# Score copies on the Vector engine: two pairs in one instruction, or each pair alone under a new planning string

## The chip, the cores and the metric

The kernel runs on one core of a Trainium2 chip. The number that counts is the device time of one execution in microseconds: 1544.43 us is the median of three runs before the change (1543.17 to 1547.52). The engines named below are TensorE (PE, its weight loads PEld), VectorE (DVE), ScalarE (ACT), GpSimd (POOL) and the queue of SyncE (SP), from which all transfers are issued.

## The reference

Four residual layers over 2048 tokens of width 512: softmax attention with 32 heads of 16, then a GELU network of width 1376, and both again with the same weights. What matters here is the exponential of the attention scores:

```python
scores = jnp.einsum("bhqd,bhkd->bhqk", q, k) * scale
p = _softmax(scores, axis=-1)
o = jnp.einsum("bhqk,bhkd->bhqd", p, v)
```

For every layer and head that is 2048 x 2048 exponentials. In tiles of 128 keys by 512 queries there are 4096 score tiles over the two attention layers.

## The kernel before, in words

**Units and segments.** The tokens are worked on in units (`build_segments`): four units of 512 queries in the first attention layer (called layer 1 in the code), and three of 512, one of 256 and two of 128 in the second (layer 3). A unit has eight groups of four heads; one unit and one group make a segment. The four heads of a group lie in the four 32-row strips of PE, so that score products (L1536) of four heads run side by side.

**Two ways to the exponential.** `flow_scores` walks over the score tiles. Groups of three and two PSUM banks alternate; ACT exponentiates a group in one instruction (L1521) into `PT`. Beside it, `take_d` and `d_solo` hand single tiles to DVE, only for the key blocks listed in `DK`. DVE adds a constant to the score and stores it as a 16-bit integer (`d_load`, L1628): read as bfloat16 bits, this is a coarse exponential. Its error is averaged out by three more copies of the same bits, shifted by 32, 64 and 96 (`SHIFT`), each multiplied with values scaled by a matching weight (`vs`). A tile on ACT therefore needs one value product (L1741), a tile on DVE four.

**The copies.** Tiles on DVE are collected in pairs (`DBATCH`). `job_d` makes the copies of a pair: first the copy shifted by 32 (L1659, 128x1024), into the second buffer of the pair, then both buffers shifted by 64 in one instruction (L1667, 128x2048), into another pair of buffers from the pool `dp`. In the kernel before, a copy task that is about to be placed looks for a second one of the same kind among those that wait. If there is one and it is ready, both are written as one instruction over two pairs (`d_join`): L1614, 128x2048 in place of two L1659, and L1615, 128x4096 in place of two L1667. For the access patterns of `both` the buffers must lie in one tensor, `bits`: 14 units of `dp` and behind them four that are `OT`, of which one pair is lent to the pool for part of the time (`LENT`). The pool is kept sorted, so that the lowest free pair is taken.

**Who sets the order.** All instructions are laid out before the kernel runs, by a planner (`Sched`) that works with durations written in the code. At each step it takes the pending task that can start first on its engine, by priority and age. A few of its settings change on the way: `Hint.ORDER` is a string with one digit for every four score groups, and each digit picks one of the sets in `MODES`. (`a` and `b` set `POST`, by which `soft` changes the priority of PE work of the GELU network.) `post_prio` gives the priority of what follows a unit's attention: 0.95 for late units, 2.2 for the others, and 0.9499 for the third unit of layer 1. Because the planner places each task where everything before has put the clock, another string gives another order from the first differing step on, on every engine and queue.

**Padding.** After the order is fixed, `refill` walks through it again and puts products with zeros (L1425, L1427, L1429) where PE would stand, so that the clock of PE is kept up.

**What follows a segment.** When the last value product of a segment is in, DVE transposes the sums (L1771), POOL or DVE divide; after eight segments the unit's output projection (L1821), the layer norm, the transposed rows `yT` (L1872), the first product of the network (L1882), one GELU session on ACT (L1934, with a table load on either side) and the second product (L1943) follow, among the score work of the next units. The first two units of layer 3 share one GELU session (`HELD`). The start of layer 3 waits for the scale of its keys (L1228 to L1232) and queries (L1262).

Of the kernel before, what the change touches and what calls it, by code (L numbers as in the profile page):

```python
# [254 lines left out]
class Task:  # L255

    __slots__ = ("eng", "ops", "prio", "cb", "seq", "mate")

    def __init__(self, eng, prio, ops):
        self.eng = eng  # L260
        self.prio = prio
        self.ops = ops
        self.cb = None
        self.seq = 0
        self.mate = None

# [12 lines left out]
class Sched:  # L279
# [80 lines left out]
    def release(self, name, slot):  # L360
        p = self.pools[name]
        if slot in p.retired:
            key = p.retired.pop(slot)
            self.mark(key)
            return
        if p.waiters:
            _, _, cb = heapq.heappop(p.waiters)
            cb(slot)
        else:
            p.free.append(slot)  # L370
            if name == "dp":
                p.free.sort()

# [74 lines left out]
    def run(self):  # L448
        while True:
# [18 lines left out]
            self.pend[t.eng].remove(t)  # L468
            both = None
            if t.mate is not None:  # L470
                lim = max(pick[0], self.P.free["dve"]) + self.LOOK["dve"]
                both = next((o for o in self.pend["dve"] if o.mate is not None and o.mate[0] == t.mate[0] and (o.mate[1] < t.mate[1]) == (o.mate[2] < t.mate[2]) and self.task_ready(o) <= lim), None)
            if both is not None:
                self.pend["dve"].remove(both)
                (fn, reads, writes, same_ok, dur, lat), more = t.ops[0], both.ops[0]
                x, y = sorted((t.mate[1:], both.mate[1:]))
                self.P.op("dve", self.join(t.mate[0], x, y), reads + more[1], writes + more[2], same_ok, dur + more[4] - SHIFT_FIXED, lat)
                for o in sorted((t, both), key=lambda o: o.mate[1:]):
                    o.cb()
            else:  # L480
                for (fn, reads, writes, same_ok, dur, lat) in t.ops:
                    self.P.op(t.eng, fn, reads, writes, same_ok, dur, lat)
                if t.cb is not None:
                    t.cb()
            if t.eng == "dve" and self.after_dve is not None:
# [5 lines left out]
AHEAD = 0.3  # L491
SHIFT_FIXED = 0.15
HOLD_REACH = 1.0
# [15 lines left out]
DBATCH = 2  # L509
DFLY = 4  # L510
DBACK = 2.0
NDP = 14
# [21 lines left out]
DOT = True  # L534
LENT = NDP + 2

# [22 lines left out]
class Builder:  # L559
# [45 lines left out]
    def alloc(self, es):  # L605
# [120 lines left out]
    def otd(self, hg):  # L726

        return [("dp", LENT + (hg - 4) // 2, w) for w in (0, 1)] if DOT and hg >= 4 else []

    def dpu(self, u):  # L730

        return self.bits[:, u, :]

    def dpp(self, u):

        return self.bits[:, u:u + 2, :]

    def both(self, a, b, o=None):

        if o is not None:  # L740
            return self.bits[:, a + o:b + o + 1:b - a, :]
        return self.bits[:, :, :].rearrange("p (u a) n -> p u (a n)", a=2)[:, a // 2:b // 2 + 1:(b - a) // 2, :]

# [866 lines left out]

    def d_join(self, kind, x, y):

        if kind == 1:
            return lambda e: e.tensor_scalar(out=self.both(x[0], y[0], 1), in0=self.both(x[0], y[0], 0), scalar1=float(SHIFT[1]), scalar2=None, op0=ALU.add)  # L1614
        return lambda e: e.tensor_scalar(out=self.both(x[1], y[1]), in0=self.both(x[0], y[0]), scalar1=float(SHIFT[2]), scalar2=None, op0=ALU.add)  # L1615

    def close_batch(self):
# [35 lines left out]
    def job_d(self, bt):  # L1653
# [4 lines left out]
        prio = lambda: 0.15 if not self.left(sg) and sg is self.segs[self.acc_seg] else 0.5 if self.left(sg) < DURGE else 2.5  # L1658
        t = Task("dve", prio(), [I(lambda e: e.tensor_scalar(out=self.dpu(u + 1)[:, 0:N], in0=self.dpu(u)[:, 0:N], scalar1=float(SHIFT[1]), scalar2=None, op0=ALU.add),  # L1659
                                     [("dp", u, w) for w in range(n)], [("dp", u + 1, w) for w in range(n)] + self.dres(u + 1), 0.150 + 0.2605e-3 * N, (), "fast")])  # L1660
        if n == DBATCH:
            t.mate = (1, u, u)
        yield t
        self.d_ready(bt, 1, u + 1, u, range(n))
        v = yield ("get", "dp", sg["i"])
        self.need2 -= 1
        t = Task("dve", prio(), [I(lambda e: e.tensor_scalar(out=self.dpp(v)[:, :, 0:N], in0=self.dpp(u)[:, :, 0:N], scalar1=float(SHIFT[2]), scalar2=None, op0=ALU.add),  # L1667
                                     [("dp", u + i, w) for i in (0, 1) for w in range(n)], [("dp", v + i, w) for i in (0, 1) for w in range(n)] + self.dres(v) + self.dres(v + 1), 0.150 + 0.521e-3 * N, (), "fast")])
        if n == DBATCH:
            t.mate = (2, u, v)  # L1670
        yield t
        for i in (0, 1):
# [391 lines left out]
    def build(self):  # L2064
# [32 lines left out]
        if DOT:  # L2097
            S_.when([("ot", 1, 0, hg) for hg in range(8)], lambda: S_.release("dp", LENT))
            S_.when([("ot", 1, self.NC - 1, hg) for hg in range(8)], lambda: S_.retire("dp", LENT, ("retd", 0)))
            S_.when([("ot", 3, 0, hg) for hg in range(8)], lambda: S_.release("dp", LENT))  # L2100
            S_.when([("ot", 3, len(self.units[3]) - 3, hg) for hg in range(8)], lambda: S_.retire("dp", LENT, ("retd", 1)))
# [3 lines left out]
        S_.join = self.d_join  # L2105
        self.P.spare = lambda: (tuple(range(6)) if self.wide and ("scores_done",) not in S_.done else ()) + ((MISCB,) if MISCB in S_.pools["mb"].free else ())
# [60 lines left out]
```

## Time and profile before

| | |
|---|---|
| median of three runs | 1544.43 us |
| the profiled execution's own time | 1543.17 us |
| its span, first to last instruction | 1541.4 us |
| granted PE clock over the span | 0.998 |
| ACT busy | 1503.9 us (98%) |
| PE busy, zero products included | 1490.7 us (97%) |
| DVE busy | 1446.3 us (94%) |
| POOL busy | 346.7 us (22%) |
| exponentials on ACT (L1521) | 1256 instructions, 1423.3 us |
| loads of score tiles on DVE (L1628) | 982 instructions, 651.6 us |

The page gives busy time, the chain that ended last and the costliest groups of instructions; a group's line reads: line of the kernel, engine, operation, output and input, count, then busy time and mean duration in ns, then the idle time of the engine just before these instructions and who ended it. A view in order of time begins with the start in us and the duration. PE's busy time is modelled, so that a full PE is not one at its peak.

### The profile page before, as it was taken

To read this page: it belongs to the slowest core of one execution; us is meant where nothing else is said; L and a number is where in the kernel's file an instruction comes from. 1 tells how busy PE (TensorE), PEld (TensorE's weight loads), DVE (VectorE), ACT (ScalarE), POOL (GpSimd) and SP (SyncE) were. 2 spreads that over 40 slices of the span, in tenths; PEclk is the share of its full clock that TensorE was granted. 3 is DMA by queue.
4 is the path that set the end of the run, shared out by engine and by line. 5 is a ranking of instruction groups with operands and counts; after the bars stand their busy time and mean duration, and the time that the engine had idled before them with its cause. 6 is when DMAs were issued, how large, how long until landed. Compare 5 with 4: busy or idle time off the path is not lost.

```text
span 1541.4 us, 41484 instructions
## 1 busy us (share of the span) xinstructions
PE 1490.7 (97%) x17809; PEld 491.4 (32%) x17809; DVE 1446.3 (94%) x2653; ACT 1503.9 (98%) x1346; POOL 346.7 (22%) x570
## 2 busy tenths in 40 slices
PE   8999999999999999999999999999999999999998
PEld 3222222232222322222222232222222222343565
DVE  8799999999999999998999898999999998998886
ACT  8999999999999999999999999999999999999997
POOL 3586421100330021301232228320001100011110
PEclk9999999999999999999999999999999999999999
DMA  6662111212312033123562233311011100111221
GB/s 166 115 151 87 35 26 32 53 35 58 80 53 63 17 66 90 50 55 72 124 106 63 65 74 71 58 26 22 22 25 29 29 19 28 43 38 43 70 60 33
DMA packets 212488, 90.57 MB, mean 59 GB/s; under 512 B 182251, under 2 KB 207184, under 8 KB 212304
## 3 DMA queue, kind: packets, MB, share of 16 engines
q1 hardware_dynamic: 212304, 87.92, 25.2%
q8 instruction: 139, 2.28, 0.6%
q14 instruction: 45, 0.37, 0.1%
HBM read 36.81 MB, written 19.48 MB: 37 GB/s over the span
## 4 chain that ended last, share of the span: by engine, by line
ACT 43%; PE 28%; DVE 23%; issue 2%; POOL 2%; DMA 1%; SPq 0%; POOLq 0%; DVEq 0%
ACT PT L1521 40%; DVE dp L1628 10%; PE ps L1536 9%; PE ps L1741 9%; PE ps L1882 3%; PE ps L1943 3%; DVE dp L1667 2%; PE ps L1016 2%; DVE dp L1615 2%; ACT h L1934 1%; DVE dp L1659 1%; DVE dp L1614 1%; DVE accT L1771 1%; PE ps L1429 1%; DVE n L1081 1%
## 5 line engine op out<-in xcount | busy, mean ns | idle before, releaser
L1521 ACT ACTIVATE PT<-ps 128x1536 bf16<-128x1536 f32 (+1 forms) x1256 | 1423.3, 1286 | 24.9 <-PE ps L1536 21.5
L1628 DVE TENSOR_SCALAR dp<-ps 128x512 uint16<-128x512 f32 x982 | 651.6, 680 | 37.9 <-PE ps L1536 34.2
L1536 PE MATMUL ps<-QT,KT 32*128 32x512 bf16 (+2 forms) x5120 | 596.3, 340 | 21.6 <-ACT PT L1521 7.2
L1741 PE MATMUL ps<-PT,V 128*17 128x512 bf16 (+2 forms) x3896 | 487.4, 339 | 1.2 <-issue 1.2
L1741 PE MATMUL ps<-dp,vs 128*17 128x512 bf16 (+2 forms) x3672 | 472.2, 339 | 0.9 <-DVE dp L1667 0.8
L1536 PEld LDWEIGHTS ps<-QT,KT 32*128 32x128 bf16 x5120 | 171.5, 91 | 535.5 <-ACT PT L1521 281.3
L1262 POOL TENSOR_SCALAR QT<-qraw,scl,qbias 128x512 bf16<-128x512 bf16 (+2 forms) x91 | 75.2, 826 | 727.9 <-PE ps L1536 721.6
L1741 PE MATMUL ps<-dp,V 128*17 128x512 bf16 (+2 forms) x1224 | 224.0, 340 | 2.1 <-DVE accT L1771 1.8
L1667 DVE TENSOR_SCALAR dp<-dp 128x2048 uint16<-128x2048 uint16 (+1 forms) x298 | 208.6, 701 | 3.2 <-PE ps L1741 0.7
L1429 PE MATMUL ps<-zw 128*32 128x448 bf16 (+17 forms) x1708 | 169.3, 326 | 1.1 <-DVE dp L1628 1.1
L1741 PEld LDWEIGHTS ps<-dp,vs 128*17 128x17 bf16 x3672 | 123.8, 89 | 120.6 <-issue 87.1
L1741 PEld LDWEIGHTS ps<-PT,V 128*17 128x17 bf16 x3896 | 125.3, 89 | 93.3 <-issue 77.7
L1659 DVE TENSOR_SCALAR dp<-dp 128x1024 uint16<-128x1024 uint16 (+1 forms) x284 | 123.2, 435 | 2.5
L1615 DVE TENSOR_SCALAR dp<-dp 128x4096 uint16<-128x4096 uint16 x98 | 122.6, 1253 | 0.1
L1427 PE MATMUL ps<-zw 32*128 32x444 bf16 (+4 forms) x364 | 113.4, 331 | 0.0
L1882 PE MATMUL ps<-yT,wf 128*128 128x512 bf16 (+5 forms) x440 | 104.5, 343 | 6.1 <-DVE dp L1615 2.2
L1016 PE MATMUL ps<-wqkv,xnT 128*128 128x512 bf16 x336 | 91.4, 382 | 1.0 <-DVE dp L1029 0.2
L1425 PE MATMUL ps<-zw 128*128 128x448 bf16 (+20 forms) x321 | 80.7, 334 | 4.9 <-DVE dp L1628 2.3
L1287 POOL TENSOR_SCALAR vs<-V 128x340 bf16<-128x340 bf16 (+2 forms) x72 | 65.7, 914 | 28.5 <-PE ps L1741 17.4
L1614 DVE TENSOR_SCALAR dp<-dp 128x2048 uint16<-128x2048 uint16 x105 | 71.7, 684 | 0.0
L1741 PEld LDWEIGHTS ps<-dp,V 128*17 128x17 bf16 x1224 | 56.5, 88 | 40.7 <-issue 21.4
L1429 PEld LDWEIGHTS ps<-zw 128*32 128x32 bf16 x1708 | 59.4, 95 | 23.2 <-DVE dp L1628 3.7
(201 smaller groups left out, 1055.0 us busy)
## 6 DMA issues: line engine op xcount, KB each, us to landing
vs<-vs_scr SPq DMA_DIRECT2D x64, 255.0 KB, 2.7
wf<-in_B_w_dram SPq DMA_DIRECT2D x90, 128.0 KB, 2.6
q_scr<-qk SPq DMA_DIRECT2D x20, 256.0 KB, 2.1
k_scr<-qk SPq DMA_DIRECT2D x12, 256.0 KB, 2.0
out_dram<-xres SPq DMA_DIRECT2D x16, 128.0 KB, 1.7
vs_scr<-vs SPq DMA_DIRECT2D x8, 255.0 KB, 3.0
xres<-in_A_x_dram SPq DMA_DIRECT2D x7, 256.0 KB, 5.4
v_scr<-vst SPq DMA_DIRECT2D x12, 136.0 KB, 1.7
```

The costliest lines, as they stand in the source:

```text
L1016: yield Task("pe", prio if c0 == 0 else min(prio, HINT.LIN2), [I(lambda e, c=c: e.matmul(self.ps[:, b, :], lhsT=xnT[:, c, :], rhs=self.wqk ...
L1427: fn = lambda e: e.matmul(self.ps[:, b, 0:w], lhsT=self.zw[32 * p:32 * p + 32, 0:128], rhs=self.zw[32 * p:32 * p + 32, 0:w], start=st, sto ...
L1429: fn = lambda e: e.matmul(self.ps[32 * p:32 * p + 32, b, 0:w], lhsT=self.zw[:, 0:32], rhs=self.zw[:, 0:w], start=st, stop=st, skip_group_c ...
L1521: S_.submit(Task("act", 1e-5 * gi, [I(lambda e, pt=pt, n=n, b0=b0: e.activation(out=self.PT[:, pt:pt + n, :], in_=self.ps[:, b0:b0 + n, :] ...
L1536: return [I(lambda e, kb=kb, i=i: e.matmul(self.ps[:, b, i * W:(i + 1) * W], lhsT=self.KT[32 * hp:32 * hp + 32, hg, kb * 128:(kb + 1) * 12 ...
L1614: return lambda e: e.tensor_scalar(out=self.both(x[0], y[0], 1), in0=self.both(x[0], y[0], 0), scalar1=float(SHIFT[1]), scalar2=None, op0= ...
L1615: return lambda e: e.tensor_scalar(out=self.both(x[1], y[1]), in0=self.both(x[0], y[0]), scalar1=float(SHIFT[2]), scalar2=None, op0=ALU.add)
L1628: self.S_.submit(Task("dve", 0.0, [I(lambda e: e.tensor_scalar(out=self.dpu(u)[:, w * 512:(w + 1) * 512], in0=self.ps[:, b, :], scalar1=BI ...
L1659: t = Task("dve", prio(), [I(lambda e: e.tensor_scalar(out=self.dpu(u + 1)[:, 0:N], in0=self.dpu(u)[:, 0:N], scalar1=float(SHIFT[1]), scal ...
L1667: t = Task("dve", prio(), [I(lambda e: e.tensor_scalar(out=self.dpp(v)[:, :, 0:N], in0=self.dpp(u)[:, :, 0:N], scalar1=float(SHIFT[2]), sc ...
L1741: ops.append((nth[j, sh] + 0.1 * i, I(lambda e, hp=hp, v=v, ap=ap[:, i * W:(i + 1) * W], first=first and i == 0, W=W: e.matmul(self.ps[32 ...
L1882: yield Task("pe", self.soft(pr if c0 == 0 else min(pr, HINT.LIN2)) if y0 == 0 else pr, [I(lambda e, c=c: e.matmul(self.ps[0:M, b, 0:W], l ...
```

## The change

Pairs are no longer joined: each copy task becomes one instruction (L1659 or L1667 alone), and `mate`, the search for a second task, `d_join` and `both` go. `OT` is a tensor of its own again, the lent pair has number 14 instead of 16, and the pool hands pairs out in the order in which they came free. The third unit of layer 1 has priority 0.95 like the fourth, and `soft` under `POST` 1 lowers every priority under 2, not only those from 0.95. `ORDER` is another string; the first 20 digits are the same.

```diff
             self.pend[t.eng].remove(t)
-            both = None
-            if t.mate is not None:
-                lim = max(pick[0], self.P.free["dve"]) + self.LOOK["dve"]
-                both = next((o for o in self.pend["dve"] if o.mate is not None and o.mate[0] == t.mate[0] and (o.mate[1] < t.mate[1]) == (o.mate[2] < t.mate[2]) and self.task_ready(o) <= lim), None)
-            if both is not None:
-                self.pend["dve"].remove(both)
-                (fn, reads, writes, same_ok, dur, lat), more = t.ops[0], both.ops[0]
-                x, y = sorted((t.mate[1:], both.mate[1:]))
-                self.P.op("dve", self.join(t.mate[0], x, y), reads + more[1], writes + more[2], same_ok, dur + more[4] - SHIFT_FIXED, lat)
-                for o in sorted((t, both), key=lambda o: o.mate[1:]):
-                    o.cb()
-            else:
-                for (fn, reads, writes, same_ok, dur, lat) in t.ops:
-                    self.P.op(t.eng, fn, reads, writes, same_ok, dur, lat)
-                if t.cb is not None:
-                    t.cb()
+            for (fn, reads, writes, same_ok, dur, lat) in t.ops:
+                self.P.op(t.eng, fn, reads, writes, same_ok, dur, lat)
+            if t.cb is not None:
+                t.cb()
...
             p.free.append(slot)
-            if name == "dp":
-                p.free.sort()
...
-    ORDER = '6178431488213042224130050030302033700020011073304410301330955937002083398440030130002450200030130000b900020559554104005025041510300311442533255001003000050793300000071500903503010300030000033043004332000204000034300444003074442000033000003055000733004099594093074053909900398000448301001020b9419803824b00195100a1010'
+    ORDER = '617843148821304222410024330100010322200010402005142300045935291731905421304450012300445404028299551400009505333207404304200030002302391015000030510104040320034300330030059090225910306350630422003320070322304130078057891b143300430303032703000430001459928b9001b338492908900532301308540020000009440105408040a010010a0211'
...
-        self.bits = t("dp", [128, NDP + 4, 1024], U16)
-        self.dp = self.bits[:, 0:NDP, :]
+        self.dp = t("dp", [128, NDP, 1024], U16)
...
-        self.OT = self.bits[:, NDP:NDP + 4, :].bitcast(BF16).rearrange("p u (a n) -> p (u a) n", n=512)
+        self.OT = t("OT", [128, 8, 512], BF16)
...
-    def d_join(self, kind, x, y):
-
-        if kind == 1:
-            return lambda e: e.tensor_scalar(out=self.both(x[0], y[0], 1), in0=self.both(x[0], y[0], 0), scalar1=float(SHIFT[1]), scalar2=None, op0=ALU.add)
-        return lambda e: e.tensor_scalar(out=self.both(x[1], y[1]), in0=self.both(x[0], y[0]), scalar1=float(SHIFT[2]), scalar2=None, op0=ALU.add)
...
-        t = Task("dve", prio(), [I(lambda e: e.tensor_scalar(out=self.dpu(u + 1)[:, 0:N], in0=self.dpu(u)[:, 0:N], scalar1=float(SHIFT[1]), scalar2=None, op0=ALU.add),
+        yield Task("dve", prio(), [I(lambda e: e.tensor_scalar(out=self.dpu(u + 1)[:, 0:N], in0=self.dpu(u)[:, 0:N], scalar1=float(SHIFT[1]), scalar2=None, op0=ALU.add),
...
-        return 1.1 if HINT.POST == 1 and 0.95 <= pr < 2 else 0.95 if HINT.POST == 2 and pr > 2 else pr
+        return 1.1 if HINT.POST == 1 and pr < 2 else 0.95 if HINT.POST == 2 and pr > 2 else pr
...
-        return 0.9499 if (L, qc) == (1, self.NC - 2) else 0.95 if L == 1 and qc >= self.NC - 2 or L == 3 and qc >= LATE3 else 2.2
+        return 0.95 if L == 1 and qc >= self.NC - 2 or L == 3 and qc >= LATE3 else 2.2
```

More of the change, by code (lines that the diff above doesn't have):

```diff
@@ L255 @@
 class Task:
-    __slots__ = ("eng", "ops", "prio", "cb", "seq", "mate")
+    __slots__ = ("eng", "ops", "prio", "cb", "seq")
     def __init__(self, eng, prio, ops):
@@ L264, in __init__ @@
         self.seq = 0
-        self.mate = None
 def I(fn, reads=(), writes=(), dur=0.3, same_ok=(), lat=None):
@@ L491 @@
 AHEAD = 0.3
-SHIFT_FIXED = 0.15
 HOLD_REACH = 1.0
@@ L534 @@
 DOT = True
-LENT = NDP + 2
 HELD = {(3, 0): (3, 1)}
@@ L726, in otd @@
     def otd(self, hg):
-        return [("dp", LENT + (hg - 4) // 2, w) for w in (0, 1)] if DOT and hg >= 4 else []
+        return [("dp", NDP + (hg - 4) // 2, w) for w in (0, 1)] if DOT and hg >= 4 else []
     def dpu(self, u):
-        return self.bits[:, u, :]
+        return self.dp[:, u, :] if u < NDP else self.OT[:, 2 * (u - NDP) + 4:2 * (u - NDP) + 6, :].rearrange("p a n -> p (a n)").bitcast(U16)
     def dpp(self, u):
[L736 to L742, printed above, removed]
+        return self.dp[:, u:u + 2, :] if u < NDP else self.OT[:, 4:8, :].rearrange("p a n -> p (a n)").bitcast(U16).rearrange("p (u n) -> p u n", u=2)
     def dres(self, s):
@@ L1658, in job_d @@
         prio = lambda: 0.15 if not self.left(sg) and sg is self.segs[self.acc_seg] else 0.5 if self.left(sg) < DURGE else 2.5
-        t = Task("dve", prio(), [I(lambda e: e.tensor_scalar(out=self.dpu(u + 1)[:, 0:N], in0=self.dpu(u)[:, 0:N], scalar1=float(SHIFT[1]), scalar2=None, op0=ALU.add),
+        yield Task("dve", prio(), [I(lambda e: e.tensor_scalar(out=self.dpu(u + 1)[:, 0:N], in0=self.dpu(u)[:, 0:N], scalar1=float(SHIFT[1]), scalar2=None, op0=ALU.add),
                                      [("dp", u, w) for w in range(n)], [("dp", u + 1, w) for w in range(n)] + self.dres(u + 1), 0.150 + 0.2605e-3 * N, (), "fast")])
-        if n == DBATCH:
-            t.mate = (1, u, u)
-        yield t
         self.d_ready(bt, 1, u + 1, u, range(n))
@@ L1666, in job_d @@
         self.need2 -= 1
-        t = Task("dve", prio(), [I(lambda e: e.tensor_scalar(out=self.dpp(v)[:, :, 0:N], in0=self.dpp(u)[:, :, 0:N], scalar1=float(SHIFT[2]), scalar2=None, op0=ALU.add),
+        yield Task("dve", prio(), [I(lambda e: e.tensor_scalar(out=self.dpp(v)[:, :, 0:N], in0=self.dpp(u)[:, :, 0:N], scalar1=float(SHIFT[2]), scalar2=None, op0=ALU.add),
                                      [("dp", u + i, w) for i in (0, 1) for w in range(n)], [("dp", v + i, w) for i in (0, 1) for w in range(n)] + self.dres(v) + self.dres(v + 1), 0.150 + 0.521e-3 * N, (), "fast")])
-        if n == DBATCH:
-            t.mate = (2, u, v)
-        yield t
         for i in (0, 1):
@@ L2097, in build @@
         if DOT:
[L2098 to L2101, printed above, removed]
+            S_.when([("ot", 1, 0, hg) for hg in range(8)], lambda: S_.release("dp", NDP))
+            S_.when([("ot", 1, self.NC - 1, hg) for hg in range(8)], lambda: S_.retire("dp", NDP, ("retd", 0)))
+            S_.when([("ot", 3, 0, hg) for hg in range(8)], lambda: S_.release("dp", NDP))
+            S_.when([("ot", 3, len(self.units[3]) - 3, hg) for hg in range(8)], lambda: S_.retire("dp", NDP, ("retd", 1)))
         S_.when([("qt", 0)], lambda: S_.spawn(self.flow_scores(), 0.0))
@@ L2104, in build @@
         S_.after_dve = self.d_solo
-        S_.join = self.d_join
         self.P.spare = lambda: (tuple(range(6)) if self.wide and ("scores_done",) not in S_.done else ()) + ((MISCB,) if MISCB in S_.pools["mb"].free else ())
```

## The prediction

> **What bounds the kernel now.** I read the page's shares first, then the chain, then the groups by form, then the Vector engine's order of time, and last the stretches in which the Scalar engine stands still. The page's head, slices and chain:
>
> ```profile
> span 1541.4 us, 41484 instructions
> PE 1490.7 (97%) x17809; PEld 491.4 (32%) x17809; DVE 1446.3 (94%) x2653; ACT 1503.9 (98%) x1346; POOL 346.7 (22%) x570
> ...
> ACT 43%; PE 28%; DVE 23%; issue 2%; POOL 2%; DMA 1%; SPq 0%; POOLq 0%; DVEq 0%
> ```
>
> Three engines are almost full, and the chain changes hands between them. No single engine can be relieved alone: each of the 4096 score tiles is exponentiated either by ACT or by DVE, so DVE time that is lost becomes ACT time. The groups by form say what a tile costs on either side:
>
> ```profile
> L1521 ACT ACTIVATE PT<-ps 128x1536 bf16<-128x1536 f32 x603 | 908.3, 1506 | 18.6 <-PE ps L1536 15.9
> L1521 ACT ACTIVATE PT<-ps 128x1024 bf16<-128x1024 f32 x652 | 699.1, 1083 | 6.3 <-PE ps L1536 5.6
> ...
> L1628 DVE TENSOR_SCALAR dp<-ps 128x512 uint16<-128x512 f32 x982 | 651.6, 680 | 37.9 <-PE ps L1536 34.2
> L1667 DVE TENSOR_SCALAR dp<-dp 128x2048 uint16<-128x2048 uint16 x292 | 205.9, 706 | 3.1 <-PE ps L1741 0.7
> L1615 DVE TENSOR_SCALAR dp<-dp 128x4096 uint16<-128x4096 uint16 x98 | 122.6, 1253 | 0.1
> L1659 DVE TENSOR_SCALAR dp<-dp 128x1024 uint16<-128x1024 uint16 x278 | 121.5, 438 | 2.5
> L1614 DVE TENSOR_SCALAR dp<-dp 128x2048 uint16<-128x2048 uint16 x105 | 71.7, 684 | 0.0
> ```
>
> L1614 and L1615 are the joined copies, L1659 and L1667 the single ones. A mean is not yet the time that the engine gives to an instruction, since neighbours overlap. The Vector engine in order of time (start, duration):
>
> ```profile
> 508.91 0.68 DVE L1614 TENSOR_SCALAR dp<-dp 128x2048 uint16<-128x2048 uint16 x1
> 509.50 0.68 DVE L1628 TENSOR_SCALAR dp<-ps 128x512 uint16<-128x512 f32 x1
> 510.10 0.68 DVE L1667 TENSOR_SCALAR dp<-dp 128x2048 uint16<-128x2048 uint16 x1
> ...
> 512.56 0.42 DVE L1659 TENSOR_SCALAR dp<-dp 128x1024 uint16<-128x1024 uint16 x1
> 512.90 0.69 DVE L1628 TENSOR_SCALAR dp<-ps 128x512 uint16<-128x512 f32 x1
> ```
>
> L1614 begins at 508.91, lasts 0.68, and the next begins at 509.50: an overlap of 0.09. L1659's is 0.08. I take 0.08 off every DVE mean. For ACT, the two exponential forms sum to 1607.4 us, while the page's group, which counts overlapped time once, has 1423.3 for 1256: 0.147 each. So a three-bank activation costs 1.359 us of ACT and a two-bank one 0.936.
>
> **The change part by part.** Durations come from the profiled execution: span 1541.4 us, its own time 1543.17, the lowest of three; the median is 1544.43, 1.3 us above it.
>
> *Unjoining.* Two singles replace each joined copy. L1614: 2 x (0.438 - 0.08) - (0.684 - 0.08) = 0.112 us, 105 times, 11.8 us. L1615: 2 x (0.706 - 0.08) - (1.253 - 0.08) = 0.079, 98 times, 7.7 us. Together 19.5 us more DVE time for the same tiles. The means hold disturbed instances. With the typical ones (0.419 and 0.684 for the singles' medians, 0.683 and 1.217 for the joined) each join is worth 0.071 us, 203 of them 14.4 us. Ends 14.4 and 19.5; I take 19.5, as the instances to come will meet the same neighbours.
>
> [...]
>
> *The new order.* The planner lays out everything anew with the new string, so I counted both instruction listings. DVE loads (L1628) go from 982 to 971; the single copies become 482 and 482 of full width with 7 and 7 half-width ones; no joined ones stay. ACT gets three more three-bank activations and one more two-bank (606 and 653), which are just the 11 tiles. So ACT: 3 x 1.359 + 0.936 = **+5.0 us**. DVE: a tile costs a load of 0.600 and half a pair of copies, (0.358 + 0.626) / 2 = 0.492, so 11 tiles give back 12.0: 19.5 - 12.0 = **+7.5 us** (by the low end, +2.4). By stage the listing loses 7 of the 11 tiles in the first layer's second unit and 4 in the second layer's fifth; the others differ by two at most.
>
> *PE.* An ACT tile needs one value product, a DVE tile four: the listing has 36 fewer, which run four at a time. One takes 0.38 in the trace, 36 / 4 x 0.38 = 3.4 us at most, while consecutive rounds start 0.22 apart, so 2.0. PE is padded with zero products (L1425, L1427, L1429), and the freed time becomes padding or idle. I count 0 and keep -2.0.
>
> *Buffers.* OT leaves the large tensor, the pair on loan from it gets another number, and a free pair is taken in order of release instead of the lowest first. Shapes and strides of the single copies stay, so no duration changes. DVE idles 3.1 us before L1667 in all; the order of reuse can take away at most that or, by the same row, add as much. I take 0, covered by a pool of 8 pairs.
>
> *Priorities.* 0.9499 becomes 0.95 for the first layer's third unit, so that its work ties with the fourth's and falls to the older task. At 681 us the third unit's GELU runs; its second products (L1943) end at 707, while the fourth unit's attention goes on for some 150 us more, so the two rarely meet. The wider condition in soft meets no other priority: the 'a' steps stand at groups 1216 to 1247, where the post work has 0.95 under both texts. Both 0. DMA counts stay at 545 rows of SP and 574 of POOL; their places move with the plan, and nothing is put past them on purpose.
>
> *Waits.* Joined copies also make others wait:
>
> ```profile
> L1741 PEld LDWEIGHTS ps<-dp,vs 128*17 128x17 bf16 x3672 | 123.8, 89 | 120.6 <-issue 87.1 <-DVE dp L1667 6.3 <-DVE dp L1615 5.1
> ```
>
> L1615 shows 5.1 us of weight-load waits, and L1614 4.4 by its own line; the single L1667 has 6.3. Weight loads run ahead of the matmuls, and matmuls behind dp lost 0.9 us in all before this line. Bounds of this gain: 0 and 9.5 us; I take 0, near the 0.9.
>
> *The stalls that a plan happens to have.* ACT's idle time of more than a microsecond in the steady part has three places:
>
> ```profile
> 707.45 16.05 ACT L1521 ACTIVATE PT<-ps 128x1024 bf16<-128x1024 f32 x14 [2.24 <-PE ps L1536]
> ```
> ```profile
> 927.09 12.76 ACT L1521 ACTIVATE PT<-ps 128x1536 bf16<-128x1536 f32 x11 [3.87 <-PE ps L1536]
> ```
> ```profile
> 1397.12 4.63 ACT L1521 ACTIVATE PT<-ps 128x1536 bf16<-128x1536 f32 x4 [2.87 <-PE ps L1536]
> ```
>
> The first (4.3 us from 691 to 707, with two small ones) is PE full of the third unit's second products after the clock had fallen to 0.58. The second is the start of the second layer, where the scale chain over DVE, POOL and PE must end first; it stays. The third is a row of yT that landed 4.8 us after its issue (others 2.5), so that PE stood 2.2 us and then had half its clock. The first and third, 7.2 us, belong to this plan; another plan drops them and brings its own. I set the exchange at 0, with ends -7.2 and +10.
>
> **Sum.** ACT +5.0 or DVE +7.5, whichever is last at each point. ACT has 37.5 us idle in the span, DVE 95, so ACT's is the floor; in stretches where DVE is busy throughout (48.20 of 48.20 us from 1107.9) DVE's part comes through. I take the middle, +6.2: 1543.2 + 6.2 = 1549.4 for an execution like the profiled one, and 1550.6 on the median, said as **1550.5**, 0.4% slower. About 0.3% is what a measurement of this kernel can tell from no change (4.6 us: below 1539.8 is faster, above 1549.1 slower).
>
> **The rivals.** *New stalls (slower still).* PE's clock falls where too little is left to multiply. In the windows around the first stall the columns are PE, weight loads, DVE, ACT, POOL, the granted clock and the DMA share and rate:
>
> ```profile
> 682.00:684.00 2.00, 1.57 (x6) 0.46 (x5) 2.00 (x4) 1.99 (x2) 0.00 (x0) 1.00 0.84 196
> 684.00:686.00 2.00, 1.77 (x17) 0.56 (x20) 2.00 (x5) 2.00 (x1) 0.00 (x0) 0.58 0.02 4
> ```
>
> Seven GELU sessions could each do this, and two places do now. Two more such places at 2.9 to 4.3 us: +6.2 + 7.2 = 1557.8. For it: the listing has 169 fewer padding products; against: the padding is planned for the new order. [...]
>
> *The plan's stalls vanish (no change).* Without the 7.2 us: 1550.6 - 7.2 = 1543.4.
>
> *Joined copies were in PE's way (faster).* One mechanism: a 1.25 us copy holds back the loads queued behind it on DVE, and the score banks with them. Its price is the 5.1 + 4.4 us of weight-load waits and the 2.2 at L1882 that the profile puts down to L1615: 11.7 in all, so 1550.6 - 11.7 = 1538.9. It decides from 6.2 us of those waits being on the path, and is faster by 0.3% from 10.8. Against it: value products lost only 0.9 us behind dp, and L1882's 2.2 has a late landing as its other candidate.
>
> **How the numbers follow.** My forecast 0.57 (0.44 of it above 1549.1, 0.13 below, since the middle lies near the bound); new stalls 0.17, all slower; stalls vanish 0.16 (0.13 no change, 0.03 faster when another gap closes too); PE freed 0.10 (0.09 faster, 0.01 not). Sums: faster 0.12, same 0.27, slower 0.61. The range leaves 0.1 on each side: below, nearly all of the faster rival; above, new stalls beyond the +10 end (1560.6): 1541 to 1561. The forecast alone spans 1544 (+5.0 less PE's 2.0 and the buffers' 3.1) to 1555 (+7.5 and 3.1).
>
> **What would show it.** Right: ACT's exponentials 606, 653 and 1, busy about 1509; DVE busy near 1454, no form wider than 128x2048; idle before L1521 near 25 us; the gap at the second layer's start still 3 to 4 us. Wrong: single copies near 0.42 and 0.68 with DVE busy unchanged (unjoining is cheaper than its means say); a granted clock under 1.00 in other 48 us stretches than those from 674 and from 1349 to 1445 (new stalls); idle before L1521 under 15 us (they vanished).

## The result and the profile after

The changed kernel takes 1541.19 us (median of 20 runs, 1539.8 to 1547.19) against 1545.88 us (20 runs, 1543.17 to 1550.93) for the kernel before on the same chip: a ratio of 0.9973, 95% interval 0.9964 to 0.9981. It is faster by 0.27%, where 0.4% slower was forecast. The gain lies inside the 0.3% that I had named as the least that a measurement can tell, but the interval excludes no change, and in two more series the ratio was 0.9961 and 0.9966 (E9 and E14 below). Both profiles are of the fastest of the 20 runs of their kernel (1543.17 and 1539.80 us).

The page of the changed kernel, its head and chain; lines are numbered differently there: L1497 is the exponential (L1521 before), L1512 the scores, L1598 the load, L1629 and L1634 the single copies (L1659 and L1667 before).

```profile
span 1538.0 us, 41184 instructions
PE 1485.6 (97%) x17604; PEld 489.9 (32%) x17604; DVE 1449.5 (94%) x2835; ACT 1508.2 (98%) x1350; POOL 333.9 (22%) x570
...
ACT 52%; PE 22%; DVE 21%; issue 2%; POOL 1%; SPq 1%; DMA 1%; POOLq 0%; DVEq 0%
...
L1497 ACT ACTIVATE PT<-ps 128x1536 bf16<-128x1536 f32 (+1 forms) x1260 | 1427.3, 1303 | 17.2 <-PE ps L1512 15.1
```

ACT is busy 4.3 us longer (1503.9 to 1508.2), as the eleven moved tiles demand, and DVE 3.2 us longer. Yet the span is 3.4 us shorter, because ACT stands still for 29.8 us in place of 37.5: -7.7 us. All of it lies before the exponentials, 17.2 us against 24.9. The chain says the same: PE's and DVE's parts shrank, ACT's grew from 43% to 52%.

The groups by form, with count, busy time, mean in ns and idle time before:

```profile
L1497 ACT ACTIVATE PT<-ps 128x1536 bf16<-128x1536 f32 x606 | 923.5, 1524 | 14.0 <-PE ps L1512 12.1
L1497 ACT ACTIVATE PT<-ps 128x1024 bf16<-128x1024 f32 x653 | 711.9, 1099 | 3.2 <-PE ps L1512 3.0
```

606 and 653 are the counts of the forecast; the durations are near those of before. Where the 7.7 us went is seen in ACT's order of time (start, duration of the run of instructions, in brackets the idle time before it). The changed kernel has one gap of more than a microsecond between 60 us and the tail:

```profile
924.69 11.41 ACT L1497 ACTIVATE PT<-ps 128x1024 bf16<-128x1024 f32 x10 [1.68 <-PE ps L1512]
```

The gaps of 1.16 and 2.24 us at 702 to 707 and the one of 2.87 us at 1397 are gone, and the one at the start of layer 3, 3.87 us before, has 1.68. With two smaller gaps near 700 the first place was 4.3 us; 4.3 + 2.9 + 2.2 = 9.4 us, of which some 1.7 us came back in gaps too short to be listed. The stretch itself, before and after, in windows of 4 us (PE, weight loads, DVE, ACT and POOL busy with their counts, granted clock, DMA share and rate), first the kernel before:

```profile
702.00:706.00 4.00, 4.00 (x33) 1.26 (x26) 3.65 (x7) 2.37 (x2) 0.00 (x0) 1.00 0.16 33
```

and the changed one:

```profile
702.00:706.00 4.00, 3.83 (x40) 0.93 (x33) 4.00 (x9) 4.00 (x4) 1.13 (x2) 1.00 0.48 92
```

Before, PE is full and ACT has 2.37 of 4 us to do. After, both ACT and DVE are full at that time. The granted clock also differs: the record of before has two falls to 0.50 between 60 us and the tail, 3.4 us each; that of the changed kernel has none.

### The profile page after: what moved, and what is told of

The parts are those of the page before. It is cut to its first block, busy times and chain, and to the rows that moved or that the text cites. A ratio compares the mean times of both kernels' runs of the same rounds, so it can differ in the third digit from the quotient of the medians.

```text
span 1538.0 us, 41184 instructions
## 1 busy us (share of the span) xinstructions
PE 1485.6 (97%) x17604; PEld 489.9 (32%) x17604; DVE 1449.5 (94%) x2835; ACT 1508.2 (98%) x1350; POOL 333.9 (22%) x570
## 4 chain that ended last, share of the span: by engine, by line
ACT 52%; PE 22%; DVE 21%; issue 2%; POOL 1%; SPq 1%; DMA 1%; POOLq 0%; DVEq 0%
ACT PT L1497 49%; DVE dp L1598 7%; PE ps L1512 7%; PE ps L1705 6%; DVE dp L1634 3%; PE ps L1907 3%; PE ps L1846 3%; DVE dp L1629 2%; ACT h L1898 2%; PE ps L992 2%; DVE st L909 1%; DVE accT L1735 1%; SPq L1780 1%; DMA OT<-ob 1%; DVE OT L1598 1%
## 5 line engine op out<-in xcount | busy, mean ns | idle before, releaser
L1497 ACT ACTIVATE PT<-ps 128x1536 bf16<-128x1536 f32 (+1 forms) x1260 | 1427.3, 1303 | 17.2 <-PE ps L1512 15.1
L1598 DVE TENSOR_SCALAR dp<-ps 128x512 uint16<-128x512 f32 x893 | 595.8, 681 | 33.4 <-PE ps L1512 30.8
L1512 PE MATMUL ps<-QT,KT 32*128 32x512 bf16 (+2 forms) x5120 | 599.5, 339 | 28.2 <-ACT PT L1497 10.9
L1705 PE MATMUL ps<-dp,vs 128*17 128x512 bf16 (+2 forms) x3318 | 433.5, 337 | 0.7 <-DVE dp L1634 0.4
L1512 PEld LDWEIGHTS ps<-QT,KT 32*128 32x128 bf16 x5120 | 172.5, 91 | 546.5 <-ACT PT L1497 307.2
L1634 DVE TENSOR_SCALAR dp<-dp 128x2048 uint16<-128x2048 uint16 (+1 forms) x399 | 277.2, 701 | 2.9 <-PE ps L1705 0.2
L1705 PE MATMUL ps<-dp,V 128*17 128x512 bf16 (+2 forms) x1128 | 202.9, 337 | 1.5 <-DVE accT L1735 1.4
L1629 DVE TENSOR_SCALAR dp<-dp 128x1024 uint16<-128x1024 uint16 (+1 forms) x450 | 187.4, 428 | 2.3
L1405 PE MATMUL ps<-zw 128*32 128x448 bf16 (+25 forms) x1466 | 163.8, 324 | 0.4 <-DVE dp L1598 0.4
L1403 PE MATMUL ps<-zw 32*128 32x444 bf16 (+2 forms) x387 | 120.5, 332 | 0.0
L1401 PE MATMUL ps<-zw 128*128 128x448 bf16 (+16 forms) x371 | 90.1, 339 | 3.4 <-DVE onec L785 2.1
L1705 PE MATMUL ps<-OT,vs 128*17 128x512 bf16 (+2 forms) x318 | 78.0, 356 | 0.0
L1735 DVE STREAM_TRANSPOSE accT<-ps 128x512 f32<-128x512 f32 (+2 forms) x96 | 59.2, 617 | 7.0 <-PE ps L1705 7.0
```

The costliest lines, as they stand in the source:

```text
L1401: fn = lambda e: e.matmul(self.ps[:, b, 0:w], lhsT=self.zw[:, 0:128], rhs=self.zw[:, 0:w], start=st, stop=st, skip_group_check=True)
L1403: fn = lambda e: e.matmul(self.ps[:, b, 0:w], lhsT=self.zw[32 * p:32 * p + 32, 0:128], rhs=self.zw[32 * p:32 * p + 32, 0:w], start=st, sto ...
L1405: fn = lambda e: e.matmul(self.ps[32 * p:32 * p + 32, b, 0:w], lhsT=self.zw[:, 0:32], rhs=self.zw[:, 0:w], start=st, stop=st, skip_group_c ...
L1497: S_.submit(Task("act", 1e-5 * gi, [I(lambda e, pt=pt, n=n, b0=b0: e.activation(out=self.PT[:, pt:pt + n, :], in_=self.ps[:, b0:b0 + n, :] ...
L1512: return [I(lambda e, kb=kb, i=i: e.matmul(self.ps[:, b, i * W:(i + 1) * W], lhsT=self.KT[32 * hp:32 * hp + 32, hg, kb * 128:(kb + 1) * 12 ...
L1598: self.S_.submit(Task("dve", 0.0, [I(lambda e: e.tensor_scalar(out=self.dpu(u)[:, w * 512:(w + 1) * 512], in0=self.ps[:, b, :], scalar1=BI ...
```

## The experiments

Three theories. *The order*: unjoining costs what the forecast said, and the new order has fewer stalls. *The short copies*: the gain is that no long copy stands in the way of loads and value products. *The clock*: the falls of the granted clock are the difference, and they follow from how much PE has to do.

Besides its time, every timed run has its mean granted clock, to three digits. Within one kernel the two go together. Over all runs on one chip I fitted a time for each kernel and one common slope against the clock. The slope is 1.36 (95% interval 0.19 either way), 1.15 (0.15) and 1.18 us (0.24) per 0.001 of mean clock on three chips. One fall of 3.413 us to 0.50 is 0.0011 over the span, so it costs 1.3 to 1.5 us. The fit also gives what each kernel would take at a mean clock of 1.000:

| chip | kernel | runs | mean clock | median us | at full clock, us |
|---|---|---|---|---|---|
| a | before | 29 | 0.9958 | 1549.78 | 1543.9 (0.9) |
| a | E1, copies split, order of before | 6 | 0.9978 | 1556.35 | 1554.0 (1.1) |
| a | E5, yT row first | 12 | 0.9966 | 1547.33 | 1542.7 (1.0) |
| a | E6, more padding | 12 | 0.9983 | 1549.26 | 1546.9 (0.8) |
| a | E7, both | 12 | 0.9977 | 1549.01 | 1545.9 (0.9) |
| b | before | 38 | 0.9968 | 1547.3 | 1543.5 (0.6) |
| b | E9, changed kernel | 5 | 0.9994 | 1540.95 | 1540.2 (1.1) |
| b | E10, changed, less padding | 10 | 0.9945 | 1546.85 | 1540.8 (1.1) |
| b | E11, narrow products | 12 | 0.9941 | 1547.55 | 1541.2 (1.1) |
| b | E12, narrow, yT row first | 12 | 0.9953 | 1545.24 | 1539.5 (1.0) |
| c | before | 23 | 0.9965 | 1549.04 | 1544.5 (1.0) |
| c | E13, changed, 66 joined | 12 | 0.9989 | 1544.7 | 1543.2 (0.8) |
| c | E14, changed kernel | 12 | 0.9987 | 1542.51 | 1541.5 (0.8) |

In brackets the half-width of the 95% interval. The fit of chip b includes the two runs each of E2 and E3. The table is an observation and not a setting of the clock; E10 below is the nearest to one. In E5 two falls came with waits of PE, of 2.7 and 2.0 us, so a part of the waits may be taken in by the slope.

**E1: the copies split, the order kept.** Every joined copy of the kernel before is issued as two single ones at the place where it stood.

```diff
     def d_join(self, kind, x, y):
-        if kind == 1:
-            return lambda e: e.tensor_scalar(out=self.both(x[0], y[0], 1), in0=self.both(x[0], y[0], 0), ...)
-        return lambda e: e.tensor_scalar(out=self.both(x[1], y[1]), in0=self.both(x[0], y[0]), ...)
+        def two(e):
+            for a, b in (x, y):
+                out, src = (self.dpu(a + 1), self.dpu(a)) if kind == 1 else (self.dpp(b), self.dpp(a))
+                ins = e.tensor_scalar(out=out, in0=src, scalar1=float(SHIFT[kind]), scalar2=None, op0=ALU.add)
+            return ins
+        return two
```

> The order of before is kept on every engine; each of the 203 joined copies is issued as its two single copies, one behind the other, at the same place. Theory 1 (the gain lies in the new order, unjoining by itself costs): 14.4 to 19.5 us more of DVE time, of which DVE's 95 us of idle time take a part, so 3 to 10 us slower than before, and the ACT gaps near 704, 925 and 1395 us stay. Theory 2 (shorter copies are the gain, since nothing waits behind a 1.25 us copy): 3 to 5 us faster, and the weight-load waits behind joined copies (9.5 us in before) fall to a few.

Measured: 1556.35 us, ratio 1.0046 (1.003 to 1.0062), so about 7 us slower, and 10.1 us (1.2) at equal clock. From its page:

```profile
PE 1475.4 (95%) x17675; PEld 492.1 (32%) x17809; DVE 1462.3 (94%) x2856; ACT 1507.1 (97%) x1346; POOL 339.3 (22%) x570
...
L1521 ACT ACTIVATE PT<-ps 128x1536 bf16<-128x1536 f32 (+1 forms) x1256 | 1426.4, 1262 | 35.2 <-PE ps L1536 31.4
```

DVE has 16.0 us more (1446.3 to 1462.3), 0.079 for each of 203 splits, and ACT's idle time before the exponentials grows from 24.9 to 35.2. The gaps of the order are where they were, in its order of time:

```profile
706.85 2.37 ACT L1521 ACTIVATE PT<-ps 128x1024 bf16<-128x1024 f32 x2 [1.17 <-PE ps L1536]
711.46 14.64 ACT L1521 ACTIVATE PT<-ps 128x1024 bf16<-128x1024 f32 x13 [2.24 <-PE ps L1536]
...
935.48 12.75 ACT L1521 ACTIVATE PT<-ps 128x1536 bf16<-128x1536 f32 x11 [3.92 <-PE ps L1536]
```

The time came out as the first theory said, 3 to 10 us. But E1 gives the short copies no chance to pay. `two` returns its last instruction, and only that one is signalled: the readers of the first pair wait for both halves, and what stood behind a joined copy on DVE stands behind both halves here. PE's weight loads for value products wait 28.9 us in all behind copies in E1, 17.9 us in the kernel before and 12.7 us in the changed kernel; behind the copies that had been joined it is 18.0 us in place of 9.5, where the second theory expected a few. The products themselves wait much less, 1.5, 0.8 and 0.4 us, so the theory of the short copies has little to gain there; E1 does not refute it. ACT is as busy as in the changed kernel (1507.1 against 1508.2); what the changed kernel has less is 18.0 us of idle time before the exponentials (35.2 against 17.2). The order, what it does to the clock, and copies that release their readers one by one can each have a part in that.

**E2 and E3: one half of the change each.** E2 is the kernel before with the search for a second copy switched off, under the old string. E3 is the kernel before, joined copies and all, under the new string. Both keep the sorted pool and the priorities of before, which no run changes by themselves.

```diff
# E2
-            if t.mate is not None:
+            if False and t.mate is not None:
# E3
-    ORDER = '61784314882130422241300500303020337000...'
+    ORDER = '61784314882130422241002433010001032220...'
```

> Before with the search for a second copy switched off, the planning string of before kept: unjoined copies under a string that belongs to another order. If the string's fit is worth little, as my sum had it, 5 to 10 us slower than before. If the order that goes with a string is worth more than the copies, far slower, 20 to 60 us, with more idle time on ACT.

> Before with its joined copies and the string of the changed kernel. If the new string were better in itself, faster than the changed kernel by the 5 to 7 us of the joined copies. If a string fits only the kernel whose order it was set for: 20 to 60 us slower than before, with more idle time on ACT.

Measured, in two runs each: 1585.79 us (ratio 1.0249, 1.023 to 1.0267) and 1582.34 us (1.0226, 1.0207 to 1.0245). The exponentials of E2, and of E3:

```profile
L1521 ACT ACTIVATE PT<-ps 128x1536 bf16<-128x1536 f32 (+1 forms) x1265 | 1442.7, 1274 | 48.1 <-PE ps L1536 43.4
```
```profile
L1521 ACT ACTIVATE PT<-ps 128x1536 bf16<-128x1536 f32 (+2 forms) x1261 | 1437.8, 1268 | 46.4 <-PE ps L1536 41.0
```

Either half alone costs 34 to 38 us, both together gain 5 to 7. Each string did badly in a kernel that it was not set for. That is five times the price of the copies in E1, so the effect of a change that goes with a new string can't be read from its copies alone.

**E5, E6, E7: the stalls of the old order, one at a time.** E5 issues the late row of `yT` ahead of a load of `vs` in the queue of SP. E6 raises the padding. E7 does both.

```diff
# E5: two neighbours in SP's list change places, the last yT row and the vs load before it
...
+        k = [k for k in range(1, len(sp) - 1) if [what(o) for o in sp[k - 1:k + 2]] == ["yT", "vs", "yT"]][-1]
+        a, b = sp[k], sp[k + 1]
...
+        sp[k], sp[k + 1] = b, a
...
# E6
-FILL_U = 0.55
+FILL_U = 0.65
```

> Before, with one pair of transfers exchanged in SP's queue: the last row of yT of the third unit of layer 3 is issued ahead of the load of vs that stood before it (at 1388.9 us). Theory 1 (PE waited at 1394 for this row, which landed 4.8 us after its issue): the row lands 2.5 us after its issue, the gap of 2.9 us on ACT and the half clock from 1394.1 go, 2.5 to 4 us faster. Theory 2 (PE waited for the joined copy L1615 that ended at 1394.4): no change within 1 us, and the gap stays.

> Before, with the padding's threshold at 0.65 in place of 0.55: more zero products in PE's planned gaps, everything else in the order of before. Theory 1 (the half clock from 684.1 us is what makes ACT wait 4.3 us until 707): the clock stays full there, 2 to 4 us faster; the fall at 1394 stays, since it follows a wait that the plan does not know. Theory 2 (PE is full of second products at 693 to 707 whatever the clock): the gap of some 4 us stays and the time changes by less than 1 us, or rises by 1 to 3 us because padding stands in the way.

> Both of the last two edits in before, joined copies kept. Theory 1 (the changed kernel is faster because its order lacks these two stalls): both gaps gone, 5 to 8 us faster than before, 1538 to 1541 us, level with the changed kernel. Theory 2 (the copies' length is the cause): within 2 us of before.

Measured: 1547.33 us (ratio 0.998, 0.9965 to 0.9995), 1549.26 (1.0002, 0.9987 to 1.0018) and 1549.01 (0.9994, 0.9983 to 1.0005). In E5 the gap at 1397 has gone; ACT works for 40 us on end across its place:

```profile
1393.96 40.23 ACT L1521 ACTIVATE PT<-ps 128x1536 bf16<-128x1536 f32 x36 [0.51 <-PE ps L1536]
```

So the wait that the profile of before put down to a joined copy was the late row. E11 below, which keeps the joined copies and the row in its old place, says so by name: there PE waits 1.8 us for the transfer of `yT`. Behind the load of `vs` the row landed after 4.8 us in the kernel before, 4.5 in E1 and E11 and 4.1 in E6; in E6 that was soon enough, and its profile has no gap there either. Putting the row in time was worth 2.5 us of the median, 1.2 (0.9) at equal clock, at or under the low end of what was expected. In E6 the fall of the clock at 684 is gone and 672 to 720 us has 1.00 throughout, yet the gaps after it stand as before:

```profile
705.18 2.37 ACT L1521 ACTIVATE PT<-ps 128x1024 bf16<-128x1024 f32 x2 [1.17 <-PE ps L1536]
709.78 50.39 ACT L1521 ACTIVATE PT<-ps 128x1024 bf16<-128x1024 f32 x44 [2.24 <-PE ps L1536]
```

They belong to the order, not to the clock. From 672 to 720 us ACT is busy 43.6 us in the kernel before, 44.5 in E1, E5 and E6, whose clock is full there, and 47.6 in the changed kernel: the fall is worth 0.9 us of it, the order 3.1. So E6 came out as its second theory said. E7 missed the gain of its first: the row's gap is gone, the gaps of 1.16 and 2.24 us stay. The extra padding raised the mean clock from 0.9958 to 0.9983 and 0.9977, and the two kernels were 3.0 us and 2.0 us slower at equal clock (1546.9 and 1545.9 against 1543.9), E7 with its row in time. The one paid for the other.

**E9 and E10: the changed kernel again, and with less padding.**

```diff
# E10, against the changed kernel
-FILL_U = 0.55
+FILL_U = 0.40
```

> The changed kernel as it is, on the chip of the runs before, beside before. Theory 1 (its order has fewer stalls): 0.997 to 0.990 of before; ACT gaps over 1.5 us only at the start of layer 3 (1.7 us) and in the tail, no gap of 1.16 and 2.24 us near its third GELU session, and at most one fall of the clock between 20 and 1530 us. Theory 3 (its one profile was lucky, both orders meet the same falls): two or three falls, and a ratio of 1.000.

> The changed kernel with the padding's threshold at 0.40 in place of 0.55, so about half of the zero products are left out; the order of all other work stays. It prices a fall of the clock in this order. If a fall costs what it seemed to in before (1 to 3 us each), every fall in its profile adds that much: with 5 to 15 falls 10 to 40 us slower than the changed kernel. If falls are covered by other work: no change.

Measured: 1540.95 us (ratio 0.9961, 0.9947 to 0.9974) and 1546.85 us (0.9996, 0.9987 to 1.0006). The exponentials of E9, and of E10:

```profile
L1497 ACT ACTIVATE PT<-ps 128x1536 bf16<-128x1536 f32 (+1 forms) x1260 | 1426.4, 1294 | 17.2 <-PE ps L1512 15.2
```
```profile
L1497 ACT ACTIVATE PT<-ps 128x1536 bf16<-128x1536 f32 (+1 forms) x1260 | 1427.1, 1301 | 26.4 <-PE ps L1512 24.1
```

E9 came out as its first theory said. E10 has the same order, the same work on ACT and DVE, and is 5.9 us slower, less than the 10 us or more that was expected. The record of E10 has six falls of 3.4 us before the tail, that of E9 none. 9.4 us between the two spans (1546.8 and 1537.4) over six falls is 1.6 us each, near the 1.3 to 1.5 of the slope; at equal clock the two kernels agree (1540.8 and 1540.2). So the clock has a part beside the order: the changed kernel keeps a clock of 0.999 at the same padding threshold that gives the kernel before 0.996 to 0.997.

**E11 and E12: less for PE where the first gap lies.** The kernel before, with the second products of the third unit 64 columns wide in place of 512 in nine of eleven parts (most of that unit's network output is left out). E12 has the `yT` row of E5 too.

```diff
-... rhs=self.w2(L, fc) ...
+... C=64 if (L, qc) == (1, 2) and 0 < fc < nf else 512 ... rhs=self.w2(L, fc)[:, 0:C] ...
```

> Before, with its order and joined copies, but the second products (L1943) of layer 1's third unit are only 64 columns wide in 9 of their 11 parts, so this unit's network output is left incomplete; 36 products lose 448 of 512 columns, some 6 us of PE time between 689 and 707 us. Theory 1 (the gaps of 1.16 and 2.24 us on ACT at 702 and 705 come of PE being full of these products, which stand ahead of the value products that free the score buffers): both gaps go and the kernel is 3 to 5 us faster than before. Rival (ACT waits there for the clock or for something else that both kernels have): the gaps stay, less than 1 us.

> The same narrow products (that unit's network output left incomplete) and the last row of yT issued ahead of vs, joined copies kept. Theory 1 (two stalls of the order are what before has more than the changed kernel): 5 to 8 us faster than before, near the changed kernel. If the falls of the clock go on elsewhere they take 1.5 us each of it.

Measured: 1547.55 us (ratio 1.0009, 0.9993 to 1.0026) and 1545.24 us (0.9986, 0.9972 to 1.0). Neither gave the gain that was expected, and E11's window shows one reason:

```profile
702.00:706.00 4.00, 4.00 (x30) 0.95 (x29) 2.68 (x6) 1.91 (x2) 0.00 (x0) 0.51 0.00 0
```

With less to multiply, the clock fell to half for 10.2 us from 696 on (13.7 us from 698 on in E12, whose profiled execution has a mean clock of 0.992; no profile of the old or the new order with the full products has a fall between 690 and 710 us). In this window PE was as full as before though its products were narrower, and ACT got 1.91 us in place of 2.37. The mean clock of the runs is 0.9941 against 0.9968. At equal clock E11 is 2.4 us (0.9) faster and E12 4.0 us (0.8), which fits a PE that was too full there and a row that came late. But that rests on the fit; in the profile the gap never closed, so that PE's second products cause it is not shown.

**E13 and E14: joined copies in the new order.** The mirror of E1. In the changed kernel, after its order is fixed, two copies of the same kind that already stand next to each other on DVE become one, where the second's inputs came before the first in the order: 66 places. E14 is the changed kernel beside it.

```diff
+    def rejoin(self):
...
+            a, b = st[i], st[i + 1]
...
+            if ka is None or kb is None or ka[0] != kb[0] or (ka[1] < kb[1]) != (ka[2] < kb[2]) or a in b.deps:
+                continue
+            if any(at[id(gone.get(id(d), d))] >= at[id(a)] for d in b.deps):
+                continue
...
+            a.fn = self.joined(ka[0], x, y)
+            a.deps = a.deps + [d for d in b.deps if d not in a.deps]
...
```

> The changed kernel, its order kept; where two copies of full width and of the same kind already stand next to each other on the Vector engine, and the inputs of the second were ready in the order before the first, they become one instruction over two pairs: 66 places. Theory (a joined copy saves about 0.08 us of the Vector engine, and in a fixed order less than half of that reaches the end, as when the old order's 203 were split: 16.0 us of work, 7.1 us of time): Vector engine busy 5.2 us less, time 2.3 us less than the changed kernel beside it, 0.15%. Rival (in the new order the Scalar engine alone is the bound, at 98%): Vector engine busy 5 us less, time the same within 0.7 us. Second rival (a joined copy holds back the value products that read the first pair): Scalar engine's idle time before the exponentials grows by 2 us or more and the time with it.

> The changed kernel as it is, beside the one with 66 joined copies on the same chip. If its order is what makes it faster: ratio 0.996 to 0.998 of the kernel before, idle time of the Scalar engine before the exponentials 17 us, no fall of the granted clock before 1530 us.

Measured: 1544.7 us (ratio to the kernel before 0.9977, 0.9964 to 0.999) and 1542.51 us (0.9966, 0.9955 to 0.9976). From the page of E13:

```profile
span 1539.3 us, 40976 instructions
...
PE 1463.3 (95%) x17470; PEld 490.4 (32%) x17604; DVE 1447.0 (94%) x2769; ACT 1507.0 (98%) x1350; POOL 335.4 (22%) x570
```

and what its weight loads for value products waited for (total us, times, longest; L1600 is the joined copy of four buffers, L1751 the value product):

```profile
PEld ps L1751 <- DVE dp L1680: 5.8, 21, 0.9
PEld ps L1751 <- DVE dp L1600: 2.9, 3, 1.6
```

DVE has only 2.1 us less (1449.1 to 1447.0), where 5.2 was expected. The time is not less but 2.2 us more: resampling the runs gives -0.4 to 3.5, and at equal clock the fit gives 1.7 (1.0). Three waits behind L1600 hold 2.9 us, the longest 1.6, and the products themselves waited 1.8 us there. So a joined copy does hold back its readers, where the plan didn't reckon with it; that is the mechanism of the faster rival, at a small size, and a sign that part of the changed kernel's gain may be the short copies'. ACT's idle time in the profiled execution (19.7 us before the exponentials against 20.5 for E14) doesn't show it, so the second rival is not confirmed by its own sign. E14 has the ratio that was expected, but not the rest: its profile has one fall of the clock, at 161 us, and 20.5 us of idle time where none and 17 were expected. E13 is no better kernel. A joined kernel with a string set for it as it now is was not tried.

## Why the prediction was wrong

*Unjoining: right in DVE time.* 203 splits, 14.4 to 19.5 us of DVE; E1 measured 16.0. I took the upper end for the neighbours' sake; the lower was nearer. (The typical durations give 0.075 a split for L1614 and 0.071 for L1615, so 14.8 us and not 14.4; the run has 0.079.)

*ACT and DVE: right in kind.* ACT +5.0, measured +4.3. DVE +7.5 (low end +2.4), measured +3.2; with E1's 16.0 in place of 19.5 it would have been 16.0 - 12.0 = 4.0.

*PE, buffers, priorities: no loss seen.* DVE idles 2.9 us before the single L1634, 3.1 before. What the pool's order and the priorities do by themselves no run shows.

*The joined copies' waits, taken as 0 between 0 and 9.5.* E1 doesn't price them, since its readers still wait for both halves. In the changed kernel the weight loads' waits behind copies fell by 5.2 us (17.9 to 12.7) and the products' by 0.4; how much of that reached the end is not shown. The 2.2 us at L1882, the third part of the rival's price, was the late row (E5). E13, 1.7 us (1.0) slower at equal clock with 66 joins, says that the pure wait isn't nothing.

*The step that failed: "another plan drops them and brings its own. I set the exchange at 0".* The 7.2 us were dropped and almost nothing came in their place; ACT's idle time fell by 7.7 us, against 4.3 us more work. The prediction gives no row or reason for an even exchange. The rival in which the stalls vanish had the mechanism, with 0.16, and its price was too low as well. That 1541.19 us lies near the low end of the range of 1541 to 1561 is luck: the sum pointed the other way. Three things were left out of the working:

- "It stays", said of the start of layer 3, was wrong. The gap is 3.87 to 3.92 us in every profile under the old order (the kernel before, E1, E5, E6, E7, E11, E12) and 1.61 to 1.69 in each of the new one (the changed kernel, E9, E10, E13, E14). What the scale chain needs is done earlier in the new order: 2.2 us.
- The profile that I read was a lucky one. It has 24.9 us of idle time before the exponentials, where those of E5, E6, E7, E11 and E12, with the same joined copies, have 29.2 to 29.6. PE's waits for transposed rows still in transfer, from 60 to 1515 us, are longer there too: 3.5 to 6.7 us in those five and E1, 1.4 in the profile of before (without the late row's 2.2), 0 to 0.8 in the four of the changed kernel (E9, E10 and E14 among them) and 3.3 in E13. In E5 PE waited 2.7 us at 791 and 2.0 us at 1438 for the rows of a unit's output projection (L1821); ACT's gaps of 3.09 us at 795 and 3.67 us at 1448 come after them, and so does the fall of the clock at 1442. No experiment set these waits.
- The falls of the clock were counted as part of two gaps. They cost time in an unchanged order too (E10, six falls and 5.9 us), and the mean clock differs from run to run of one kernel (0.992 to 1.000 for the kernel before): in the steady part of their profiles the kernel before has them at 684 and 1394 us, E5 at 793 (two steps) and 1442, E6 at 1153 and 1440, E7 at 796 (two steps). The runs of before have a mean clock of 0.996 to 0.997 on three chips, those of the changed kernel 0.999: on chips b and c 0.0026 and 0.0022 apart, which at 1.15 and 1.18 us per 0.001 is 3.0 and 2.6 us. I started from a profiled execution with 0.998.

At equal clock the changed kernel is still 3.4 us (1.2) and 3.1 us (1.0) faster than before (E9, E14), though E1 is 10.1 us slower. So 13 us lie between E1 and the changed kernel. They hold the new order with its pool and priorities, the eleven moved tiles, and copies that release their readers one by one; the runs do not part these.

The forecast of 25 us of idle time before the exponentials was right for an even exchange; 17.2 is near the bound of 15 that I had named for vanished stalls.

What stays open: which of the moved steps brings the scale chain forward (the gap at the start of layer 3 is 3.86 us in E2 and 3.31 in E3, so neither half closes it alone), how much of the 13 us is the short copies', and whether PE's second products or another order of the same work made the gaps at 702 to 707.

## What to carry to other kernels

Separate the price of an edit from the price of the order that comes with it: issue the edit in the old order (E1, here 7 to 10 us slower), then read the rest as a change of its own (here 13 us faster at equal clock). See to it that the readers wait in such a run for what they would wait for in the changed kernel; in E1 they did not. Where a plan is laid out anew, the list of the old plan's stalls, from more than one profile, is what a plan that suits the kernel can gain; E2 and E3, whose plans did not suit, brought more than they dropped. Setting "drops them and brings its own" at zero is a guess that needs a reason. And write the mean clock beside each time: two kernels 6 us apart can be equal at full clock (E9 and E10), and two of the same time can differ by 3 us (before and E6).

## What the runs showed of the hardware

In these profiles the clock fell to 0.50 in steps of 3.413 us, one to four in a row (three in E11, four in E12), and almost the same order had them in other places: E5 keeps the order of before but for two neighbours on one queue, and its falls are at 793 and 1442 us in place of 684 and 1394. The first came during a wait of PE of 2.7 us for rows in transfer, the second soon after one of 2.0 us. In the kernel before, the fall at 1394 began before a wait of PE of 2.2 us was over.

Work taken away from PE was lost to the clock here: with an eighth of the columns in part of the products, the clock was at 0.51 for 702 to 706 us (E11), and from 672 to 720 us ACT was busy no longer than before (43.7 against 43.6 us; 41.2 in E12). Padding with zero products worked the other way and had its own price: a setting of 0.65 in place of 0.55 raised the mean clock by 0.0025 and cost 3.0 us at equal clock (E6), while 0.40 in the new order cost 0.0049 of mean clock and 5.9 us (E10).
